# Output projection of the last two tile pairs by seven products, with the sums of w_o made in the second pass of keys and values

## The chip, the cores and the metric

The kernel runs on one core of a Trainium2 chip. TensorE (PE) multiplies, VectorE (DVE), ScalarE (ACT) and GpSimd (POOL) work on elements, and SyncE (SP) issues nearly all DMA transfers of the part that is changed. Each engine takes its own instructions in order, and engines wait for each other by semaphores. The metric is the device time of one execution in microseconds (us), as the median of several runs; lower is better.

## The reference

With B = 1, S = 2048 rows, D = 1024, H = 32 heads of 32 and a hidden width of 3584, all in float32:

```python
xn = layernorm(x)
q, k, v = heads(xn @ wqkv)
phi_q, phi_k = ([softmax(p), softmax(-p)] over the features of a head, p = q @ w_phi or k @ w_phi)
kv, z = sum over rows of phi_k^T v, sum over rows of phi_k          # per head
o = (phi_q @ kv) / (phi_q . z + 1e-6)
s = o.reshape(S, D) @ wo                                            # the output projection
B = (silu(xn @ w1) * (xn @ w3)) @ w2
return x + s * silu(B)
```

## The kernel before

**Products.** Every large product is made of float32 operands that are split in two: a cast to the rounded type (`hi`, on ACT) and the rest (`lo`, on DVE), both by `split`. A product of 128 rows by 512 columns takes three matmuls for each 128 of depth, `PASSES` = hi·hi, hi·lo, lo·hi. The hidden layer, the queries, keys and values and the w2 product go one step further: the matrices are cut in 2 x 2 blocks and multiplied in the manner of Strassen and Winograd, seven products of blocks in place of eight:

```python
ORDER = (("b", "A11", "B11"), ("a", "A12", "B21"), ("b", "S2", "T2"), ("c", "S1", "T1"),
         ("b", "S3", "T3"), ("c", "S4", "B22"), ("b", "A22", "T4"))
LAST = {"a": "A12", "b": "A22", "c": "S4"}
```

The first letter is the PSUM bank that a product adds to; `S1 = A21 + A22`, `S2 = S1 - A11`, `S3 = A11 - A21`, `S4 = A12 - S2`, and `T1` to `T4` are the like sums of the blocks of the other matrix (`b_sums` on POOL makes T2 and T3's source first). A bank is read between two products that add to it, so a product may have to wait for the copy of the sum so far. The 16 row tiles are worked in eight pairs.

**Stages, by the trace.** Layernorm and the hidden layer end at about 1132 us. Then come three passes over the eight pairs (`heads` twice, `queries` once; matmuls at L932, a pair takes 20.6 us): the first and second halves of keys and values, c=0 (1133 to 1297) and c=1 (1297 to 1464), and the queries, c=2 (1464 to 1617). In a pass each pair has seven products, and between them `steps()` issues side work: loads of the next pair's operands (`reload`), and in c=0 from the fifth product on `split_wo`, which loads the 16 blocks of w_o (128 x 512 each, two rooms, each with two places for a raw block and its split form), splits them and stores them to `wo_d`. A row `ev` is a feature or value tile of a pass, `k0` the copy of A11's part of a pair. The w2 product goes from 1617 to 2156 (L1338).

**The last stage** (2156 to 2351) is the output projection, in plain products: `wos[c, k]` holds the 16 split blocks of w_o, and for each of eight pairs b `half_out` makes the four quarters (row tile a, column half c), 24 matmuls each into one of three banks `pm`. Around these stand, for the pairs after it: `load_e`, `swap` (transposes of the features on DVE), `weigh`, `add_up`, `factors` and `weights` (denominators on POOL and DVE), `heads_out` (L1309, 128 small matmuls that make the next pair's o, transposed, in two PSUM tiles `po0` and `po1` of two banks each) and `operand` (casts and low parts of `po` to `oT`). `result(m, p)` handles the m-th quarter: multiply by the gate (L1484, DVE), add x (L1485, POOL, in the last quarter DVE), store, and load of the gate and x for three quarters later (`load_gx`, tile `gx`). Rows `late` are blocks of w_o that stand in a ring of other weights. Code is written out in the order in which each engine is to run it, and SP's queue takes its loads and stores in that order.

In the rows, a line number is that of the file's kernel; after the change it is 1 higher up to L1163, 25 higher in the second pass's loop, and 27 higher in the last stage up to L1492.

Of the kernel before, what the change touches and what calls it, by code (L numbers as in the profile page):

```python
# [17 lines left out]
P = 128  # L18
# [10 lines left out]
def tile_kernel(ctx: ExitStack, tc: tile.TileContext, x, wkT, wqT, wv, wphi, wo, w1, w3, w2, out):  # L29
# [8 lines left out]
    def close(*names):  # L38
        for name in names:
            open_pools.pop(name).__exit__(None, None, None)  # L40
# [39 lines left out]
    s_d = dram.tile([4, P, 2, P], F, name="s_d")  # L80
    zr_d = dram.tile([P, 2, 256], F, name="zr_d")
    wo_d = [[dram.tile([P, 2, 512], F, name=f"wo_d{c}_{k}") for k in range(ND)] for c in range(2)]
    w2_d = [{n: dram.tile([P, 2, 2, 512], F, name=f"w2_d{kb}{n}") for n in BNAMES} for kb in range(NKB)]
    kv_d = [dram.tile([P, 8, DH], F, name=f"kv_d{c}") for c in range(2)]
    kvu_d = dram.tile([P, 16, DH], F, name="kvu_d")
# [1065 lines left out]
    def split_wo(step):  # L1151

        if step == 0:
            wso["room"] = [big.tile([P, 8, 512], F, name="room", tag=f"big{j}") for j in range(2)]
        for m in range(16):
            room, at_ = wso["room"][m % 4 // 2], 3 * (m % 2)
            raw_w, two = room[:, at_], room[:, at_ + 1:at_ + 3].bitcast(R)
            c, k = m // 8, m % 8
            if step == 2 * m:
                nc.sync.dma_start(raw_w, wo[k * P:(k + 1) * P, c * 512:(c + 1) * 512])  # L1160
            elif step == 2 * m + 3:
                split(two[:, 0], two[:, 1], raw_w)
            elif step == 2 * m + 5:  # L1163
                nc.sync.dma_start(wo_d[c][k], two.bitcast(F))

    close("ps2")
    ps = pool("ps", 2, space=PSUM)
    BANKS = {"a": 2, "b": 3, "c": 2}
# [2 lines left out]
    for c in range(3):  # L1171
        wbn = {}
        if c == 2:
            in_order(ENG.SP, ENG.PE)
            close("spare")
            bpa = pool("ra", 1, side="right")
        for i in range(len(pairs)):
            nxt, end = {}, i + 1 == len(pairs)

            def steps():  # L1180
                for j in range(7):
                    if c == 0 and 4 <= 7 * i + j < 40:
                        split_wo(7 * i + j - 4)
                    if j == 0:
                        if i + 2 == len(pairs) and c < 2:
                            for m in range(2):
                                wbn.update(fetch(c + 3, m))
                        if c == 2 and i == 6:
                            nxt.update(reload(7, ANAMES[:3]))
                            ahead[0, 0] = load_h(0, 0)  # L1190
                            nxt.update(reload(7, ANAMES[3:]))
                        elif not (end and c == 2):
                            nxt.update(reload((i + 1) % len(pairs)))
                        if c == 2 and i in (1, 2):
# [295 lines left out]
    def weights(b):  # L1490

        scale(b, 0, nc.vector)  # L1492
        scale(b, 1, nc.gpsimd)

    load_gx(0)
    load_gx(1)
    load_e(2, 1)
    gate(*pairs[-1])
    load_gx(2)
    last = None  # L1500
    for b in range(NB):
        p0 = half_out(oT, 0, 0)
        if b == 0:
            add_up(1, 1)
# [27 lines left out]
        if b < 2:  # L1532
            if b == 0:
                heads_out([po[a // 2][:, a % 2] for a in range(4)])
            add_up(b + 2, 1)
            nxt = [operand(0, [(0, po[0]), (2, po[1])])]
            factors(b + 2)
            weights(b + 2)
            if b == 0:
                result(2, p2)  # L1540
            nxt.append(operand(1, [(0, po[0]), (2, po[1])]))
        else:
            if b + 2 < NB:
                weights(b + 2)
            if b + 1 < NB:
                nxt = [operand(t, [(0, po[0]), (2, po[1])]) for t in range(2)]
        if b + 2 < NB:
            for c in range(2 if b == 0 else 1):
                swap(b + 2, c)
                load_e(b + 4, c)  # L1550
# [5 lines left out]
        if b + 3 < NB:  # L1556
            add_up(b + 3, 0)
        oT = nxt
    result(4 * NB - 1, last)
    in_order()  # L1560
    close("ps4", "rb", "acc", "q", "work", "small", "misc", "ra", "rw", "edge_r", "edge_l")

# [37 lines left out]
```

## Time and profile before

| what | value |
|---|---|
| median of 3 runs | 2360.53 us (2357.38 to 2361.70) |
| the profiled execution | 2357.35 us, span 2355.2 us |
| PE busy | 2330.3 us, 99% of the span, 13298 matmuls |
| weight loads (PEld) | 1924.1 us, 82%, beside the matmuls |
| DVE busy | 1755.1 us, 75% |
| ACT busy | 861.2 us, 37% |
| POOL busy | 759.4 us, 32% |
| DMA | 588.93 MB, 250 GB/s in the mean |
| matmul clock granted | 1.0 in the run |

The span is the time from the first to the last record of the execution. An engine's busy time is that of its records; PE's matmuls overlap, so what one of them is worth is read from the starts of many in a row and not from the mean duration of a record. A row of a wait names the engine that waited, the tile that it was about to make, and the instruction or transfer that came last. Rows in order of time have the start, the length, the engine, the line, the operation, output<-input, and at the end in brackets the idle time ahead and its releaser.

### The profile page before, as it was taken

Reading aid. Unit: us, or ns where it says so; the run is one execution under the profiler, and the core shown is the slowest. Engines: PE = TensorE matmul, PEld = TensorE weight load, DVE = VectorE, ACT = ScalarE, POOL = GpSimd, SP = SyncE. Lnnn points to the kernel's source line nnn. Section 1 sums busy time; section 2 is a strip of 40 time slices with the busy share of each in tenths; the row PEclk is TensorE's granted clock in tenths of the full one; section 3 lists DMA queues with packets and bytes.
Section 4 is the critical chain, followed back from the end, with each engine's and each line's share of the span. In section 5 each row is a group of like instructions: output and inputs, shape, how many; then the busy total and the mean of one; then the engine's idle time right before and its main releaser. Section 6 shows DMA issues by size and latency. Waiting matters only on the chain. (4 is left out here: it accounts for less than half of the span.)

```text
span 2355.2 us, 35868 instructions
## 1 busy us (share of the span) xinstructions
PE 2330.3 (99%) x13298; PEld 1924.1 (82%) x13298; DVE 1755.1 (75%) x2531; ACT 861.2 (37%) x1535; POOL 759.4 (32%) x571
## 2 busy tenths in 40 slices
PE   7999999999999999999999999999999999999999
PEld 6888888888888888888888888888888888888877
DVE  8777877784688878885566656797678778888883
ACT  6544545443445444453221211234422222243100
POOL 2333545452455555552000000231011111115872
PEclk9999999999999999999999999999999999999999
DMA  5667699987877777776998877999444443367754
GB/s 188 212 217 248 217 331 334 310 295 224 271 269 256 256 272 280 264 265 225 367 337 341 320 243 272 356 346 314 150 148 167 179 179 124 118 253 294 246 184 133
DMA packets 320558, 588.93 MB, mean 250 GB/s; under 512 B 25728, under 2 KB 158336, under 8 KB 317696
## 3 DMA queue, kind: packets, MB, share of 16 engines
q1 hardware_dynamic: 305600, 571.96, 69.7%
q10 hardware_dynamic: 14784, 14.68, 1.8%
q8 instruction: 105, 1.72, 0.3%
q14 instruction: 69, 0.57, 0.1%
HBM read 380.76 MB, written 206.32 MB: 249 GB/s over the span
## 5 line engine op out<-in xcount | busy, mean ns | idle before, releaser
L344 DVE TENSOR_TENSOR bo<-rw,bo 128x512 fp32r<-128x512 f32 x332 | 309.0, 931 | 144.0 <-ACT bo L340 142.0
L1348 POOL TENSOR_TENSOR acc<-acc,u 128x512 f32<-128x512 f32 x48 | 63.0, 1312 | 450.6 <-ACT u L1347 442.9
L1338 PE MATMUL bankb<-bo,as 128*128 128x512 f32 x816 | 201.1, 389 | 0.4 <-DMA bo<-w_d0T 0.4
L340 ACT CAST bo<-rw 128x512 fp32r<-128x512 f32 x332 | 199.0, 617 | 5.5 <-DMA rw<-in_w 3.5
L1338 PEld LDWEIGHTS bankb<-bo,as 128*128 128x128 f32 x816 | 153.0, 188 | 32.6 <-DMA bo<-w_d0T 0.8
L1465 PE MATMUL pm<-wos,oT 128*128 128x512 f32 x720 | 166.9, 390 | 0.0
L703 PE MATMUL bankc<-op0S,bo 128*128 128x512 f32 x672 | 163.3, 392 | 0.9 <-DVE bo L344 0.5
L703 PE MATMUL bankb<-op0S,bo 128*128 128x512 f32 x672 | 162.8, 391 | 1.2 <-DVE bo L344 0.6
L703 PE MATMUL bankb<-op0A,bo 128*128 128x512 f32 x672 | 163.1, 392 | 0.0
L703 PE MATMUL bankb<-op1S,bo 128*128 128x512 f32 x672 | 161.4, 389 | 0.0
L703 PE MATMUL bankb<-op1A,bo 128*128 128x512 f32 x672 | 161.4, 389 | 0.0
L703 PE MATMUL bankc<-op1S,bo 128*128 128x512 f32 x672 | 161.4, 389 | 0.0
L1465 PEld LDWEIGHTS pm<-wos,oT 128*128 128x128 f32 x720 | 134.6, 188 | 30.6 <-issue 2.9
L703 PEld LDWEIGHTS bankc<-op1S,bo 128*128 128x128 f32 x672 | 126.2, 188 | 26.1
L703 PEld LDWEIGHTS bankb<-op1S,bo 128*128 128x128 f32 x672 | 126.2, 188 | 26.1
L703 PEld LDWEIGHTS bankb<-op1A,bo 128*128 128x128 f32 x672 | 126.2, 188 | 26.1
L703 PEld LDWEIGHTS bankb<-op0S,bo 128*128 128x128 f32 x672 | 125.3, 188 | 27.1 <-DVE bo L344 0.9
L703 PEld LDWEIGHTS bankc<-op0S,bo 128*128 128x128 f32 x672 | 125.1, 188 | 27.2 <-DVE bo L344 0.8
L1338 PE MATMUL bankc<-bo,as 128*128 128x512 f32 x576 | 146.2, 389 | 0.0
L703 PEld LDWEIGHTS bankb<-op0A,bo 128*128 128x128 f32 x672 | 125.0, 188 | 25.4
L129 POOL TENSOR_TENSOR rw<-rw 128x512 f32<-128x512 f32 x56 | 81.6, 1457 | 149.1 <-DMA rw<-in_w 129.2
L1350 DVE TENSOR_TENSOR acc<-bankb,acc 128x512 f32<-128x512 f32 x152 | 104.3, 686 | 32.7 <-PE bankb L1338 28.6
(262 smaller groups left out, 4708.4 us busy)
## 6 DMA issues: line engine op xcount, KB each, us to landing
rw<-in_w SPq DMA_DIRECT2D x224, 256.0 KB, 3.6
hr<-h_d SPq DMA_DIRECT2D x56, 512.0 KB, 4.0
xoS<-xo_d0S SPq DMA_DIRECT2D x48, 512.0 KB, 8.1
xoS<-xo_d1S SPq DMA_DIRECT2D x48, 512.0 KB, 6.8
xoA<-xo_d0A SPq DMA_DIRECT2D x36, 512.0 KB, 7.6
xoA<-xo_d1A SPq DMA_DIRECT2D x36, 512.0 KB, 6.1
e<-e_d SPq DMA_DIRECT2D x32, 512.0 KB, 5.6
h_d<-h SPq DMA_DIRECT2D x56, 256.0 KB, 4.6
```

The lines of the kernel that those rows point to most:

```text
L129: nc.gpsimd.tensor_sub(b12, b22, b12)
L340: nc.scalar.copy(bos[k, n][:, 0], raw_b(k, n).rearrange("p (k n) -> p k n", n=P))
L344: nc.vector.tensor_sub(b[:, 1], raw_b(k, n).rearrange("p (k n) -> p k n", n=P), b[:, 0].bitcast(F))
L703: nc.tensor.matmul(bank, bt[:, w, kk], aos[tb][an][:, u, kk], start=an in ("A11", "A12", "S1") and n == 0, stop=LAST[b] == an and n == 11, ...
L1338: nc.tensor.matmul(bank[b], t[:, u, pos + k], bos[kb, bn, k][:, w], start=first and n == 0, stop=LAST[b] == an and n == 5, skip_group_chec ...
L1348: nc.gpsimd.tensor_add(c, c, u)
L1350: nc.vector.tensor_add(c, pb, c)
L1465: nc.tensor.matmul(p, oT[a][k // 4][:, u, k % 4], wos[c, 4 * (k % 2) + k // 2][:, w], start=n == 0, stop=n == 23)
```

## The change

The last two pairs, b=6 and b=7, are projected by seven products of 12 matmuls (`product7`, depth 512, three passes) in place of four quarters of 24. The loop over pairs ends at b=5.

- `sum_wo`, in the second pass (c=1) from its fifth product on, one step to a product: for each of four blocks of the depth it loads four blocks of w_o, makes T2, T3, T1, T4 (POOL), splits each into `two`, one buffer of a room (`room[:, 5:7]`), and stores it to the new `wt_d`. Two rooms take turns by block.
- In the last stage 16 loads bring `wt_d` back: T2 to a ring and T1 and T3 to tiles of `accp` after b=4, after b=5 and in b=6, and T4 over w_o's own blocks of B12 (`reuse_b12`), which the seven products don't need.
- `raw_o` copies o from `po` to four tiles `ro` on ACT (L1547), `one` splits an operand to `o7`, `sums_o` makes S3, S1, S2 and the split of S2 on DVE, `rest_o` the splits of S1, S3, S4 and A22.
- Banks: three `pm` banks for b=6; for b=7 the tile `po0` holds the banks "b" and "a" and `po1` the bank "c".
- A product's end: A11's, S2's and S1's sums so far are copied to `part` (ACT, L1594); A12's, S3's and S4's are added to that (DVE) and go through `put`, which does what `result` does.

```diff
+    def sum_wo(step):
+        if step == 0:
+            wso["sums"] = [big.tile([P, 8, 512], F, name="room", tag=f"big{j}") for j in (5, 6)]
+        for k in range(4):
+            room, at_ = wso["sums"][k % 2], step - 8 * k
+            b11, b12, b21, b22, t2 = (room[:, j] for j in range(5))
+            two = room[:, 5:7].bitcast(R)
+            if at_ == 0:
...
+                        nc.sync.dma_start(room[:, 2 * a + c], wo[r0:r0 + P, c * 512:(c + 1) * 512])
+            elif at_ == 3:
+                b_sums(b11, b12, b22, t2)
+            elif at_ == 5:
+                nc.gpsimd.tensor_sub(b11, b22, t2)
+                nc.gpsimd.tensor_sub(b21, b21, t2)
+            for j, (n, src) in enumerate((("T2", t2), ("T3", b12), ("T1", b11), ("T4", b21))):
+                if at_ == 4 + 2 * j:
+                    split(two[:, 0], two[:, 1], src)
+                elif at_ == 5 + 2 * j:
+                    nc.sync.dma_start(wt_d[n][k], two.bitcast(F))
...
+                    if c == 1 and 4 <= 7 * i + j < 40:
+                        sum_wo(7 * i + j - 4)
...
+    def raw_o():
+        o = {}
+        for n, t, m in (("A11", 0, 0), ("A12", 0, 1), ("A21", 1, 0), ("A22", 1, 1)):
+            o[n] = work.tile([P, 4, P], F, name="ro", tag="w")
...
+            for c in range(2):
+                nc.scalar.copy(r5[:, :, c], src[:, :, c, t])
+        return o
...
+    def sums_o(ops, o):
+        o["S3"] = work.tile([P, 4, P], F, name="ro", tag="w")
+        nc.vector.tensor_sub(flat(o["S3"]), flat(o["A11"]), flat(o["A21"]))
+        o["S1"], o["S2"], o["S4"] = o["A21"], o["A11"], o["A12"]
+        nc.vector.tensor_add(flat(o["S1"]), flat(o["A21"]), flat(o["A22"]))
+        nc.vector.tensor_sub(flat(o["S2"]), flat(o["S1"]), flat(o["A11"]))
+        one(ops, o, "S2")
+    def rest_o(ops, o):
+        one(ops, o, "S1")
+        one(ops, o, "S3")
+        nc.vector.tensor_sub(flat(o["S4"]), flat(o["A12"]), flat(o["S2"]))
+        one(ops, o, "S4")
+        one(ops, o, "A22")
...
+    def product7(b, an, bn, ops, bank):
...
+                nc.tensor.matmul(bank, ops[an][:, u, k], w4[:, w], start=first and n == 0,
+                                 stop=LAST[BANK[an]] == an and n == 11, skip_group_check=True)
...
+        if an in ("A11", "S2", "S1"):
+            part[an] = work.tile([P, 512], F, name="part", tag="h1", bufs=2)
+            nc.scalar.copy(part[an], bank)
+        elif an == "A12":
+            nc.vector.tensor_add(part["A11"], bank, part["A11"])
+            put(4 * b, part["A11"])
...
-    for b in range(NB):
+    for b in range(NB - 2):
...
+        if b == 4:
+            for k in range(4):
+                load_t("T2", k, None)
+            load_t("T1", 0, None)
+            for k in (1, 2):
+                load_t("T1", k, k - 1)
+        if b == 5:
+            for n, k, tag in (("T1", 3, 2), ("T3", 0, 3), ("T3", 1, 8), ("T3", 2, 9)):
+                load_t(n, k, tag)
+    b = NB - 2
+    sums_o(ops, o)
...
+        product7(b, an, bn, ops, banks7[bk])
+        if an == "A11":
+            swap(b + 1, 1)
+            result(4 * b - 1, last)
+            load_gx(4 * b + 3)
+            rest_o(ops, o)
+            load_t("T3", 3, 10)
+            for k in range(4):
+                reuse_b12("T4", k)
+        elif an == "S1":
+            heads_out([po[a // 2][:, a % 2] for a in range(4)])
+            o2, ops2 = raw_o(), {}
+            one(ops2, o2, "A11")
+            one(ops2, o2, "A12")
+    sums_o(ops2, o2)
+    rest_o(ops2, o2)
+    b, last2 = NB - 1, [ps.tile([P, 2, 512], F, name=f"po{m}", bufs=1) for m in range(2)]
+    banks7 = {"b": last2[0][:, 0], "a": last2[0][:, 1], "c": last2[1][:, 0]}
+    for _, an, bn in ORDER:
+        product7(b, an, bn, ops2, banks7[BANK[an]])
```

Three places in the order of instructions show where the new work stands. ACT in the second pass, in the third pair: `k0` and the copies of `bankb` and `bankc` empty PE's banks, `ACTIVATE` is the exponential of the features. Before:

```order
L945 COPY k0_11536<-bankb_11523 128x512
L117 ACTIVATE ev_11472<-ev_11472 128x1024
L955 COPY ev_11642<-bankb_11523 128x16x32
L117 ACTIVATE ev_11642<-ev_11642 128x1024
L960 COPY ev_11668<-bankc_11655 128x16x32
L945 COPY k0_11732<-bankb_11719 128x512
```

And after the change, with `room` the cast of a sum:

```order
L946 COPY k0_11575<-bankb_11562 128x512
L118 ACTIVATE ev_11501<-ev_11501 128x1024
L94 CAST room_11307<-room_11307 128x512
L956 COPY ev_11686<-bankb_11562 128x16x32
L94 CAST room_11308<-room_11308 128x512
L94 CAST room_11307<-room_11307 128x512
L118 ACTIVATE ev_11686<-ev_11686 128x1024
L961 COPY ev_11714<-bankc_11701 128x16x32
L94 CAST room_11307<-room_11307 128x512
L946 COPY k0_11790<-bankb_11777 128x512
```

Four casts stand between the copies that PE's banks need. Three of them write the one buffer of room 11307, so each of these comes after the store of the one before.

ACT at the end of the program, where the last operands are made. Before:

```order
L93 CAST oT_20072<-po0_18512 128x2x128 x2
L93 CAST oT_20073<-po1_18513 128x2x128 x2
L93 CAST oT_20082<-po0_18512 128x2x128 x2
L93 CAST oT_20083<-po1_18513 128x2x128 x2
L93 CAST oT_20292<-po0_18512 128x2x128 x2
L93 CAST oT_20293<-po1_18513 128x2x128 x2
L93 CAST oT_20302<-po0_18512 128x2x128 x2
L93 CAST oT_20303<-po1_18513 128x2x128 x2
L1596 UNCONDITIONAL_BRANCH
```

After the change, from the first two copies of b=7's o on:

```order
L1547 COPY ro_20419<-po0_18610 128x2x128 x2
L1547 COPY ro_20422<-po1_18611 128x2x128 x2
L94 CAST o7_20425<-ro_20413 128x512
L94 CAST o7_20428<-ro_20416 128x512
L94 CAST o7_20491<-ro_20413 128x512
L94 CAST o7_20494<-ro_20419 128x512
L94 CAST o7_20497<-ro_20487 128x512
L94 CAST o7_20501<-ro_20416 128x512
L94 CAST o7_20504<-ro_20422 128x512
L1594 COPY part_20521<-po0_20507 128x512
L1594 COPY part_20551<-po0_20507 128x512
L1594 COPY part_20565<-po1_20508 128x512
```

The seven casts, of A11, A12, S2, S1, S3, S4 and A22, all stand ahead of the copy of A11's part out of the tile `po0`.

PE at the end, with its waits. Before, the last pair:

```order
L1465 MATMUL pm<-wos,oT 128x512 [waits DVE_49,Activation_49]
L1465 MATMUL pm<-wos,oT 128x512 x2
L1465 MATMUL pm<-wos,oT 128x512 [waits Activation_49]
L1465 MATMUL pm<-wos,oT 128x512 x8
L1465 MATMUL pm<-wos,oT 128x512 [waits Activation_49]
L1465 MATMUL pm<-wos,oT 128x512 x2
L1465 MATMUL pm<-wos,oT 128x512 [waits Activation_49]
L1465 MATMUL pm<-wos,oT 128x512 x8
L1465 MATMUL pm<-wos,oT 128x512 [waits DVE_49]
L1465 MATMUL pm<-wos,oT 128x512 x20
L1465 MATMUL pm<-late,oT 128x512 x3
```

After, the first five products of b=7 (A11, A12, S2, S1, S3):

```order
L1589 MATMUL po_20507<-wos,o_20425 128x512 [waits PE_49,Activation_49]
L1589 MATMUL po_20507<-wos,o_20425 128x512 x11
L1589 MATMUL po_20507<-wos,o_20428 128x512 [waits Activation_49]
L1589 MATMUL po_20507<-wos,o_20428 128x512 x11
L1589 MATMUL po_20507<-late,o_20491 128x512 [waits DVE_49]
L1589 MATMUL po_20507<-late,o_20491 128x512 x8
L1589 MATMUL po_20507<-wt,o_20491 128x512 x3
L1589 MATMUL po_20508<-wt,o_20494 128x512 [waits PE_49]
L1589 MATMUL po_20508<-wt,o_20494 128x512 x11
L1589 MATMUL po_20507<-wt,o_20497 128x512 [waits Activation_49]
L1589 MATMUL po_20507<-wt,o_20497 128x512 x11
```

A12's first matmul (`o_20428`) waits for ACT, and S2's (`o_20491`) for DVE; the tile `po_20507` holds the banks of both.

More of the change, by code (lines that the diff above doesn't have):

```diff
@@ L82, in tile_kernel @@
     wo_d = [[dram.tile([P, 2, 512], F, name=f"wo_d{c}_{k}") for k in range(ND)] for c in range(2)]
+    wt_d = {n: [dram.tile([P, 2, 512], F, name=f"wt_d{n}_{k}") for k in range(4)] for n in ("T1", "T2", "T3", "T4")}
     w2_d = [{n: dram.tile([P, 2, 2, 512], F, name=f"w2_d{kb}{n}") for n in BNAMES} for kb in range(NKB)]
@@ L1164, in split_wo @@
                 nc.sync.dma_start(wo_d[c][k], two.bitcast(F))
+    def sum_wo(step):
[6 more added lines that the diff above has]
+            if at_ == 0:
+                for a in range(2):
+                    r0 = (4 * (k % 2) + 2 * a + k // 2) * P
+                    for c in range(2):
[10 more added lines that the diff above has]
+                    nc.sync.dma_start(wt_d[n][k], two.bitcast(F))
     close("ps2")
@@ L1493, in weights, with load_t, reuse_b12, b_of @@
         scale(b, 1, nc.gpsimd)
+    wt = {}
+    def load_t(n, k, tag):
+        t = ring("wt") if tag is None else accp.tile([P, 2, 512], R, name="wt", tag=f"acc{tag}")
+        nc.sync.dma_start(t.bitcast(F), wt_d[n][k])
+        wt[n, k] = t
+    def reuse_b12(n, k):
+        t = wos[1, 4 * (k % 2) + k // 2]
+        nc.sync.dma_start(t.bitcast(F), wt_d[n][k])
+        wt[n, k] = t
+    def b_of(bn, k):
+        if bn in wt_d:
+            return wt[bn, k]
+        return wos[int(bn[2]) - 1, 4 * (k % 2) + 2 * (int(bn[1]) - 1) + k // 2]
@@ new lines, in raw_o, with one @@
+    def raw_o():
+        o = {}
+        for n, t, m in (("A11", 0, 0), ("A12", 0, 1), ("A21", 1, 0), ("A22", 1, 1)):
+            o[n] = work.tile([P, 4, P], F, name="ro", tag="w")
+            r5 = o[n].rearrange("p (b c) (r u) -> p b c r u", c=2, u=4)
+            src = po[m].rearrange("p b (c t u r) -> p b c t r u", c=2, t=2, u=4)
+            for c in range(2):
+                nc.scalar.copy(r5[:, :, c], src[:, :, c, t])
+        return o
+    def one(ops, o, n):
+        ops[n] = quad("o7")
+        split(ops[n][:, 0], ops[n][:, 1], o[n])
@@ new lines, in put @@
+    def put(m, src):
+        (b, a, c), t = halves[m], gx.pop(m)
+        nc.vector.tensor_mul(t[:, 0], src, t[:, 0])
+        (nc.vector if m + 2 == len(halves) else nc.gpsimd).tensor_add(t[:, 0], t[:, 0], t[:, 1])
+        r0 = SETS[b][a] * P
+        nc.sync.dma_start(out[r0:r0 + P, c * 512:c * 512 + 512], t[:, 0])
+        if m + 4 < len(halves):
+            load_gx(m + 4)
+    part = {}
+    def product7(b, an, bn, ops, bank):
+        first = an in ("A11", "A12", "S1")
+        n = 0
+        for k in range(4):
+            w4 = b_of(bn, k)
+            for u, w in PASSES:
+                nc.tensor.matmul(bank, ops[an][:, u, k], w4[:, w], start=first and n == 0,
+                                 stop=LAST[BANK[an]] == an and n == 11, skip_group_check=True)
+                n += 1
+        if an in ("A11", "S2", "S1"):
[4 more added lines that the diff above has]
+            put(4 * b, part["A11"])
+        elif an == "S3":
+            nc.vector.tensor_add(part["S1"], bank, part["S1"])
+            put(4 * b + 3, part["S1"])
+        elif an == "S4":
+            nc.vector.tensor_add(part["S2"], bank, part["S2"])
+            put(4 * b + 1, part["S2"])
+        else:
+            put(4 * b + 2, bank)
@@ L1544, in tile_kernel @@
                 weights(b + 2)
-            if b + 1 < NB:
+            if b + 3 < NB:
                 nxt = [operand(t, [(0, po[0]), (2, po[1])]) for t in range(2)]
+            else:
+                o, ops = raw_o(), {}
+                one(ops, o, "A11")
+                one(ops, o, "A12")
         if b + 2 < NB:
@@ L1558, in tile_kernel @@
         oT = nxt
-    result(4 * NB - 1, last)
+        if b == 4:
[9 more added lines that the diff above has]
+    sums_o(ops, o)
+    banks7 = {}
+    for _, an, bn in ORDER:
+        bk = BANK[an]
+        if bk not in banks7:
+            banks7[bk] = ps.tile([P, 512], F, name="pm", tag="mm", bufs=3)
+        product7(b, an, bn, ops, banks7[bk])
[5 more added lines that the diff above has]
+            load_t("T3", 3, 10)
+            for k in range(4):
+                reuse_b12("T4", k)
[8 more added lines that the diff above has]
+    banks7 = {"b": last2[0][:, 0], "a": last2[0][:, 1], "c": last2[1][:, 0]}
+    for _, an, bn in ORDER:
+        product7(b, an, bn, ops2, banks7[BANK[an]])
     in_order()
```

## The prediction

> **What bounds the kernel now.** I read the page first, then the waits of PE, then the order of time in the two places that the change touches.
>
> ```profile
> span 2355.2 us, 35868 instructions
> PE 2330.3 (99%) x13298; PEld 1924.1 (82%) x13298; DVE 1755.1 (75%) x2531; ACT 861.2 (37%) x1535; POOL 759.4 (32%) x571
> PE 31%; DMA 1%; issue 0%; DVE 0%; POOL 0%; ACT 0%; POOLq 0%; DVEq 0%; ACTq 0%
> PE bankc L932 <- issue: 1.2, 1, 1.2
> ```
>
> PE is busy for 99% of the span, the chain of waits is PE's, and outside the opening no wait of PE is over 1.2 us (last row). So a matmul less is worth its own time, and a wait that is put on PE costs all of its length. The profiled execution took 2357.35 us, 2.15 above its span and 3.18 below the median of the runs, 2360.53; sums below are made against this execution and then set on the median. 0.2% is 4.7 us, about what a measurement of this kernel tells from no change.
>
> The last two pairs, b=6 and b=7, in order of time:
>
> ```profile
> 2304.24 10.36 PE L1465 MATMUL pm<-wos,oT 128*128 128x512 f32 x45
> 2315.21 2.76 PE L1309 MATMUL po<-et,kvt 32*32 32x256 f32 x128
> 2317.90 10.50 PE L1465 MATMUL pm<-wos,oT 128*128 128x512 f32 x45
> 2328.91 10.36 PE L1465 MATMUL pm<-wos,oT 128*128 128x512 f32 x45
> 2339.79 10.36 PE L1465 MATMUL pm<-wos,oT 128*128 128x512 f32 x45
> 2349.99 0.84 PE L1465 MATMUL pm<-late,oT 128*128 128x512 f32 x3
> 2350.93 0.69 DVE L1484 TENSOR_TENSOR gx<-pm,gx 128x512 f32<-128x512 f32 x1 [4.75 <-PE pm L1465]
> 2351.65 0.69 DVE L1485 TENSOR_TENSOR gx<-gx 128x512 f32<-128x512 f32 x1
> ```
>
> 48 matmuls (45 on `wos`, 3 on `late`) lie between 2328.91 and 2339.79: 0.2267 us each, 2.72 for a product of 12. PE doesn't pause, and `heads_out` of the last pair moves the next start from 2315.12 (2304.24 plus 48 x 0.2267) to 2317.90: 2.78.
>
> **The matmuls saved.** Two pairs by seven products of 12 take 168 matmuls in place of 192: 24 x 0.2267 = **5.44 us less**. That is the most that the change can give; nothing after the last product changes (multiply, add, store).
>
> **The last pair's new waits.** The order shows the place: ACT's seven casts of the last pair stand ahead of its copy of A11's part. The banks of this pair are two tiles `po0` (products "b" and "a") and `po1` ("c"); the built program makes the first matmul of A12 wait for ACT and the first of S2 for DVE, and their semaphore counts are those of that copy and of A12's own eviction, since all four touch the tile `po0`. S2 would have to wait for the copy anyway (same bank); A12, a product ahead of it, waits because of the tile alone. What the copy waits for, in durations:
>
> ```profile
> 1355.15 2.88 PE L932 MATMUL bankc<-op3B,xoS 128*128 128x512 f32 x12
> 1357.87 2.88 PE L932 MATMUL bankb<-op3T,xoA 128*128 128x512 f32 x12
> 1358.07 0.69 DVE L964 TENSOR_TENSOR ev<-bankc,ev 128x512 f32<-128x512 f32 x1 [1.96 <-PE bankc L932]
> 1297.57 0.69 DVE L111 TENSOR_REDUCE mm<-bankb 128x16 f32<-128x512 f32 x1 [2.03 <-PE bankb L932]
> 1298.18 0.68 DVE L112 TENSOR_REDUCE mm<-bankb 128x16 f32<-128x512 f32 x1
> L93 ACT CAST as<-s 128x512 fp32r<-128x512 f32 x15 | 9.3, 620 | 43.4 <-DVE s L1143 43.4
> L94 DVE TENSOR_TENSOR as<-s,as 128x512 fp32r<-128x512 f32 x15 | 10.4, 692 | 0.3
> L344 DVE TENSOR_TENSOR bo<-rw,bo 128x512 fp32r<-128x512 f32 x332 | 309.0, 931 | 144.0 <-ACT bo L340 142.0
> ```
>
> A product's eviction starts 2.92 after the product (1355.15 to 1358.07); DVE's operations on 128x512 start 0.60 apart, 0.70 where one needs the one before; a cast takes 0.62 and a low part 0.69 (0.93 in the row where POOL also works). Call the start of b=6's A22 zero. Six products and `heads_out` lie before it, so it is 2304.24 + 16.32 + 2.78 = 2323.34. A11 of b=7 goes from 2.72, A12 wants 5.44. On DVE A22's multiply starts at 2.92, then S3 at 3.5, S1 at 4.1, S2 at 4.8 to 5.5 (it needs S1). ACT casts S2 from 5.55 to 6.17; DVE makes the low parts of S2, S1, S3 from 6.2, 6.8, 7.4 and the sum S4 from 8.0 to 8.7. ACT, which has cast S1 and S3 meanwhile, casts S4 from 8.75, A22 from 9.3, and copies A11's part from 9.8 to 10.4. So A12 starts at 10.45 and not 5.44: **5.0 us of waiting**. Its eviction starts 2.92 later, at 13.4, and ends at 14.1; S2 starts there, not at 13.2: **0.9 more**. S1, S3, S4 and A22 follow at 16.8, 19.5, 22.3, 25.0, and the last multiply at 27.9, on the clock of the trace 2351.2 against 2350.93: **+0.3**. With POOL's additions beside DVE's first sums (0.93 for 0.69, twice) it is +0.8; if DVE and ACT overlap more than I let them, -0.5. I take +0.4, since as many rows lie at 0.69 as POOL has additions there.
>
> **b=6 itself** doesn't wait, by the same steps. Raw copies and casts of its first two operands stand where the casts of `operand` stood:
>
> ```profile
> 2293.35 0.37 ACT L93 CAST oT<-po 128x256 fp32r<-128x256 f32 x1 [15.98 <-PE po L1309]
> 2318.03 0.37 ACT L93 CAST oT<-po 128x256 fp32r<-128x256 f32 x1 [17.00 <-PE po L1309]
> 2318.89 0.65 ACT L93 CAST oT<-po 128x256 fp32r<-128x256 f32 x2 [0.49 <-DVE oT L94]
> ```
>
> Eight of these 0.28 apart (two take 0.65) and two casts end 3.5 after `heads_out`; DVE has the first sum of S2 ready by 2304.6, S2's product wants it at 2309.7. For b=7 the same work ends on DVE at 2322.3, and S3's eviction behind it at 2322.9, under A22's start of 2323.34: cover 0.4, and 0.3 of waiting if the low parts take 0.93. I set 0.
>
> **The 16 loads of the sums** (512 KB each) go on SP's queue, seven after b=4's results, four after b=5's, five in b=6; PE needs them from 2309.7. The latest is the fourth of T3: it stands behind a load that has to wait until result 23 is stored, since both use one buffer. That result's multiply comes behind the transposes, at about 2307.7; then
>
> ```profile
> L1485 POOL TENSOR_TENSOR gx<-gx 128x512 f32<-128x512 f32 x31 | 39.7, 1294 | 54.9 <-DVE gx L1484 35.9 <-DMA gx<-in_x 16.1 <-DMA e<-e_d 2.0
> out<-gx SPq DMA_DIRECT2D x32, 256.0 KB, 2.3
> wo_d<-room SPq DMA_DIRECT2D x16, 512.0 KB, 8.2
> wo_d<-room SPq DMA_DIRECT2D x1, 512.0 KB, 2.8
> ```
>
> 0.7 + 1.3 + 2.3 and two issues: it is issued at 2312.5 and lands 2.8 to 8.2 later, 2315 to 2320.7, wanted at 2317.9 + 9 x 0.2267 = 2319.9. At the long end it is 0.8 late; the queue is idle then, so I take 0.
>
> **The second pass (c=1)** gets 16 splits (16 casts of 0.62 on ACT, 16 low parts on DVE), 16 POOL sums, 16 loads and 16 stores. Room for the work there is:
>
> ```profile
> 1236.00:1256.00 20.00, 20.00 (x211) 16.46 (x210) 12.77 (x18) 3.92 (x6) 0.26 (x2) 1.00 0.95 361
> 1380.00:1400.00 20.00, 20.00 (x211) 16.47 (x210) 12.31 (x17) 3.79 (x5) 0.26 (x2) 1.00 0.59 182
> ACT room L93 <- DMA room<-in_wo: 24.0, 12, 5.8
> ```
>
> (Columns: window, its length, busy PE, PEld, DVE, ACT, POOL, clock, DMA share, GB/s.) In a pair's 20.6 us DVE works 12.3 and ACT 3.8; the new work adds about 2.2 and 2 to a pair. The first pass carries 16 splits of `wo` already, with ACT waiting 24.0 us for their loads, and PE lost there only the 1.2 us of the first fence. But the new splits write one buffer per room, so a cast has to wait until the split before it is stored, and ACT takes its instructions in order. Where that hurts is the third pair:
>
> ```profile
> 1343.42 1.06 ACT L117 ACTIVATE ev<-ev 128x1024 f32<-128x1024 f32 x1
> 1346.26 0.34 DVE L120 RECIPROCAL r<-r 128x32 f32<-128x32 f32 x1
> 1350.45 1.06 ACT L117 ACTIVATE ev<-ev 128x1024 f32<-128x1024 f32 x1 [0.72 <-DVE ev L115]
> 1352.70 0.59 ACT L960 COPY ev<-bankc 128x512 f32<-128x512 f32 x1 [1.19 <-PE bankc L932]
> 1163.74 0.45 SPq L1160 DMA_DIRECT2D room<-in_wo  x1
> 1174.78 0.32 SPq L1164 DMA_DIRECT2D wo_d<-room  x1
> ```
>
> T3 of the first block is cast after the exponential of 1343.42, its low part made after the reciprocal of 1346.26, its store issued near 1347.4. T1's cast waits for that store; behind it stand the exponential (1.06) and the copy of S1's bank (0.59), which the product of 1355.15 needs. So a landing over 1355.15 - 1347.4 - 0.62 - 1.06 - 0.59 = 5.4 us makes PE wait. In the first pass the stores took 8.2 in the median, but those that SP had been waiting to issue (nothing issued from 1163.74 to 1174.78) landed in 2.8; the new ones are of this kind. The Trainium skill ("DMA: Bandwidth & Descriptors", Queues, rings and completion order) says that each engine consumes a ring's descriptors in order; the 2.8 beside 8.2 agrees, and by it a store in an idle queue isn't held up by the loads issued behind it. Bounds: 0, and three such places (T1 of the first three blocks) at 8.2 - 5.4: 8.4. I take 0.3, nearest to the 2.8.
>
> **Sum:** -5.44 + 5.9 of waits, which is +0.4 with the rounding of the ends, +0.3 = +0.7, on the median 2361.2.
>
> **Rivals.**
> Slower: *stores on ACT's path* in the second pass, as just priced: from a landing of 5.4 us on, up to +8.4, with the rest 2369.6. For it speaks the 8.2; against it the 2.8 and that DMA is at 0.59 there.
> *PE's clock.* A wait of 5 us might let the clock fall. The trace has:
>
> ```profile
> 10.81 1.95 PE L225 MATMUL pt<-ident,xt 128*128 128x128 f32 x8 [10.81 <-DVE xt L219]
> 14.52 5.05 PE L225 MATMUL pt<-ident,xt 128*128 128x128 f32 x24 [1.76 <-DVE xt L219]
> 36.09 1.03 PE L225 MATMUL pt<-ident,x_room 128*128 128x128 f32 x8
> 38.35 1.09 PE L225 MATMUL pt<-ident,x_room 128*128 128x128 f32 x8 [1.23 <-ACT xf L230]
> ```
>
> After 10.8 us idle, 32 transposes took 7.0 us where 8 take 1.03 later (32: 4.1), while 1.23 us of waiting changed nothing. Half speed for a while costs at most the 2.9 between them: 2364. A wait of 5.0 lies between 1.23 and 10.8. The Trainium skill ("TensorE: Matmul & The Clock Gate", Part 1) has the array at half clock after an idle window of about 3.4 us; its windows run freely, so a wait of 5.0 would hold a whole one in about half of the cases (an estimate from that page).
> *Faster:* A12 doesn't wait for the copy after all. Then S2 waits from 8.16 to 10.45, 2.3 in place of 5.9: -3.1, 2357.7; with no wait at all -5.4, 2355.1. Against it stand the semaphore counts.
>
> **Chances.** The waits take the gain, within -1 and +2.5: 0.56. The clock falls as well: 0.18, about 2364. Stores on ACT's path: 0.18, most of it beyond 4.7. A12 free: 0.08, half of that without S2's wait. Faster by over 0.2% needs nearly all of the 5.44: 0.04; slower: 0.18 and a little of the clock's case, 0.2; within: 0.76. The range goes from A12 free (2357.5) to the stores' middle (2367).
>
> **What would show it.** In the profile after: 24 matmuls fewer at the end; in b=7 PE idle 4.5 to 5.5 us ahead of A12's product, released by ACT's copy, and 0.9 ahead of S2's, released by DVE; the last multiply within 1 us of 27.6 behind b=6's A22; no wait of PE over 1 us between 1297 and 1464. Waits of PE there for ACT's copies, or matmuls 0.43 apart behind the long wait, would make the prediction wrong upwards; no wait ahead of A12 downwards.

## The result and the profile after

The changed kernel takes 2377.39 us (median of 4 runs, 2375.47 to 2381.58) against 2359.26 before (2357.38 to 2361.70): the ratio is 1.0079, interval 1.0061 to 1.0096. It is slower by 18.1 us where I forecast 2361.2 and a range up to 2367.0. The profiled execution took 2376.87, 1.77 above its span.

The first rows of the page:

```profile
span 2375.1 us, 36003 instructions
PE 2332.7 (98%) x13274; PEld 1922.9 (81%) x13274; DVE 1787.2 (75%) x2559; ACT 880.1 (37%) x1571; POOL 786.4 (33%) x587
```

The 24 matmuls are gone (13298 to 13274), yet PE is busy 2.4 us longer: some of its matmuls ran slow. The waits of PE (what waited, released by what: us in total, times, longest), without those of the opening that were there before:

```profile
PE po L1589 <- ACT part L1594: 5.9, 1, 5.9
PE pm L1589 <- DMA wt<-wt_dT: 4.0, 1, 4.0
PE pkv L918 <- DVE ev L126: 3.6, 1, 3.6
PE bankc L933 <- ACT d L1074: 1.7, 2, 1.5
PE bankb L933 <- DMA xoA<-xo_d0A: 1.5, 1, 1.5
...
PE bankb L933 <- DVE ev L963: 0.9, 2, 0.5
...
PE po L1589 <- DVE part L1596: 0.9, 1, 0.9
```

Before, no wait outside the opening was over 1.2 us. The first and the last row are the two that I forecast. To see what each is worth I took the length of each stage from the start of its first matmul to that of the next stage (the last: to the end of PE's last matmul):

| stage | before | after | difference |
|---|---|---|---|
| up to the second pass | 1297.37 | 1297.05 | -0.3 |
| second pass (c=1) | 166.95 | 174.00 | +7.05 |
| queries (c=2) | 154.56 | 159.48 | +4.92 |
| w2 product | 537.32 | 536.17 | -1.15 |
| pairs b=0 to 5 | 148.04 | 148.07 | 0.0 |
| pairs b=6 and 7 | 46.59 | 55.91 | +9.32 |

The sum is +19.85, and the spans differ by 19.9. (The w2 product takes 536.2 to 537.5 in all the runs below, whatever the kernel; the second pass 174.0 here and 173.3 to 173.5 in three more runs with the same sums.) The last two pairs, in order of time:

```profile
2328.43 2.34 PE L1589 MATMUL pm<-wt,o 128*128 128x512 f32 x9
2334.77 1.65 PE L1589 MATMUL pm<-wt,o 128*128 128x512 f32 x3 [4.01 <-DMA wt<-wt_dT]
2336.22 2.96 PE L1589 MATMUL pm<-wos,o 128*128 128x512 f32 x9
...
2342.44 2.88 PE L1589 MATMUL po<-wos,o 128*128 128x512 f32 x12
2351.24 4.68 PE L1589 MATMUL po<-wos,o 128*128 128x512 f32 x12 [5.92 <-ACT part L1594]
2356.77 2.35 PE L1589 MATMUL po<-late,o 128*128 128x512 f32 x9 [0.85 <-DVE part L1596]
2358.95 6.29 PE L1589 MATMUL po<-wt,o 128*128 128x512 f32 x27
```

S3 of b=6 stands after 9 of its 12 matmuls, for T3's fourth load; A12 of b=7 waits 5.92 for the copy of A11's part. Behind each of the two waits matmuls are slow: A12's 12 take 4.68 where A11's took 2.88. From the start of b=6 (2314.77) to that of the last product (2367.80) lie 53.03 us; 13 products of 2.72 and `heads_out` of 2.78 are 38.15. So 14.9 were lost, against 5.4 saved: 10.8 in waits and 4.1 around them, about 3.5 of that in slow matmuls (the rest is the overlap of a product's start with the end of the one before, which a wait takes away).

In the second pass the largest loss stands in the fourth pair:

```profile
1355.20 2.88 SPq L599 DMA_DIRECT2D xoS<-xo_d0S  x4
1360.29 0.80 SPq L1189 DMA_DIRECT2D wt_dT<-room  x2
1370.24 0.62 ACT L94 CAST room<-room 128x512 fp32r<-128x512 f32 x1 [4.73 <-DMA wt_dT<-room]
1370.89 0.69 DVE L95 TENSOR_TENSOR room<-room 128x512 fp32r<-128x512 f32 x1 [3.52 <-ACT room L94]
1371.50 0.35 DVE L121 RECIPROCAL r<-r 128x32 f32<-128x32 f32 x1
1372.31 1.21 DVE L126 TENSOR_TENSOR ev<-ev,r 128x1024 f32<-128x1024 f32 x1
1373.66 0.76 PE L918 MATMUL pkv<-ev 128*32 128x34 f32 x64 [3.60 <-DVE ev L126]
1374.35 4.62 PE L933 MATMUL bankc<-op3T,xoS 128*128 128x512 f32 x12
```

A cast (T3 of the second block) waits for the store of T2, the second of the two issued from 1360.29 on, behind 2 MB of `xoS` loads. VectorE's low part waits for the cast, the reciprocal and multiply of the features stand behind the low part on VectorE, and PE wants the features. Two rows of the transfers give the landing of the stores: the 16 of the pass in the median, and the median of the two issued at 1360. The second of these, issued at 1360.66, is the one that the cast waits for: it took 9.6.

```profile
wt_dT<-room SPq DMA_DIRECT2D x16, 512.0 KB, 4.2
wt_dT<-room SPq DMA_DIRECT2D x2, 512.0 KB, 9.0
```

The queries' pass has no line of the change in it. But here, unlike in the last stage, VectorE, ScalarE and GpSimd run in an order that a planner makes from its own estimates of times, and it made another one: of 196 instructions of VectorE in this pass 27 stand elsewhere, of ScalarE's 86 five, of GpSimd's 32 two. VectorE in the first pair, before and after the change:

```profile
1483.05 0.69 DVE L1078 TENSOR_TENSOR d<-bankc,d 128x512 f32<-128x512 f32 x1
1483.78 0.69 DVE L996 TENSOR_REDUCE tops<-d 128x16 f32<-128x512 f32 x1
1484.73 1.22 DVE L1006 TENSOR_REDUCE s_all<-eq 128x32 f32<-128x1024 f32 x1 [0.26 <-ACT eq L1001]
1485.87 0.68 DVE L997 TENSOR_REDUCE mm<-d 128x16 f32<-128x512 f32 x1
```

```profile
1489.79 0.69 DVE L1079 TENSOR_TENSOR d<-bankc,d 128x512 f32<-128x512 f32 x1
1491.47 1.22 DVE L1007 TENSOR_REDUCE s_all<-eq 128x32 f32<-128x1024 f32 x1 [0.99 <-ACT eq L1002]
1492.60 0.68 DVE L997 TENSOR_REDUCE tops<-d 128x16 f32<-128x512 f32 x1
1493.20 0.68 DVE L998 TENSOR_REDUCE mm<-d 128x16 f32<-128x512 f32 x1
```

`tops` now stands behind a sum that waits for ScalarE, so the minimum, from which GpSimd and ScalarE go on, comes 3.41 behind the addition from `bankc` in place of 2.82. A pair later PE waits 1.50 for ScalarE's copy of `bankc`, and 1.50 for a load of `xoA` that SyncE issued later.

### The profile page after: what moved, and what is told of

It is laid out like the page before. It is cut to its first block, busy times and chain, and to the rows that moved or that the text cites. A ratio compares the mean times of both kernels' runs of the same rounds, so it can differ in the third digit from the quotient of the medians.

```text
span 2375.1 us, 36003 instructions
## 1 busy us (share of the span) xinstructions
PE 2332.7 (98%) x13274; PEld 1922.9 (81%) x13274; DVE 1787.2 (75%) x2559; ACT 880.1 (37%) x1571; POOL 786.4 (33%) x587
## 5 line engine op out<-in xcount | busy, mean ns | idle before, releaser
L1365 PEld LDWEIGHTS bankc<-bo,as 128*128 128x128 f32 x576 | 108.1, 188 | 22.5
L1492 PE MATMUL pm<-wos,oT 128*128 128x512 f32 x540 | 125.3, 391 | 0.0
L1377 DVE TENSOR_TENSOR acc<-bankb,acc 128x512 f32<-128x512 f32 x152 | 104.2, 686 | 26.4 <-PE bankb L1365 22.6
```

What stands on the lines that cost most here:

```text
L1365: nc.tensor.matmul(bank[b], t[:, u, pos + k], bos[kb, bn, k][:, w], start=first and n == 0, stop=LAST[b] == an and n == 5, skip_group_chec ...
L1377: nc.vector.tensor_add(c, pb, c)
L1492: nc.tensor.matmul(p, oT[a][k // 4][:, u, k % 4], wos[c, 4 * (k % 2) + k // 2][:, w], start=n == 0, stop=n == 23)
```

## The experiments

All are compared with the kernel before on the same chip. "Second pass", "queries" and "last two pairs" are differences in length from the profile of before, as in the table above.

**Which part costs.** Two runs split the change. The sums alone are the changed kernel's `sum_wo` in the kernel before, with `wt_d` stored and not read:

```diff
+                    if c == 1 and 4 <= 7 * i + j < 40:
+                        sum_wo(7 * i + j - 4)
```

> The kernel before, with the sums of w_o made, split and stored in the second pass and never read; the projection is as before. Theory: the loss ahead of the last stage is all due to this work: the second pass 7.0 us longer (the largest single wait of PE 3.6 in the fourth pair, behind a cast that waits for a store), the queries' pass 4.8 longer, the w2 product 1.1 shorter: 2359.3 + 10.7 = 2370. Rival: the loads and operands of the last stage share the blame (through the queue or through the order of instructions): under 5 us in all, 2364 or less.

2366.78 against 2357.08, ratio 1.0038 (1.0023 to 1.0053), so 9.7 us. Second pass +6.3, queries +3.9. The second part alone:

```diff
-                    if c == 1 and 4 <= 7 * i + j < 40:
-                        sum_wo(7 * i + j - 4)
+    wt_d = {n: [wo_d[m // 2][4 * (m % 2) + k] for k in range(4)] for m, n in enumerate(("T1", "T2", "T3", "T4"))}
```

> The changed kernel without the sums of w_o: the 16 loads of the last stage read split blocks of w_o in their place, so the projection of the last two pairs has wrong weights and the same instructions. Theory: nothing changes ahead of the last stage (within 0.5 us), and the last two pairs lose 14.9 us in waits and slow matmuls (T3's load 4.0, A11's copy 5.9, A12's eviction 0.9, clock 4.1) against 5.4 saved: 2359.3 + 9.4 = 2368.7. Rival: T3's late load follows from the second pass being late; then it is not there, and the run takes 2363.

2367.55 against 2357.08, ratio 1.0040 (1.0025 to 1.0055): 10.5 us. Second pass +0.1, queries -0.2, last two pairs +10.6, with T3's wait of 3.4 and A12's of 5.9. The two parts add up (9.7 + 10.5 = 20.2 against 18.1 +- 4), and the last stage's loss doesn't come from the passes ahead of it.

**What holds the second pass.** Two edits of the sums alone that take the store away from ScalarE. In the first each sum has places of its own in the room:

```diff
-            for j, (n, src) in enumerate((("T2", t2), ("T3", b12), ("T1", b11), ("T4", b21))):
+            for j, (n, src, lo, hi) in enumerate((("T2", 4, 5, 6), ("T3", 1, 1, 7), ("T1", 0, 0, 4), ("T4", 2, 2, 3))):
...
-                    split(two[:, 0], two[:, 1], src)
+                    split(room[:, hi].bitcast(R), room[:, lo].bitcast(R), room[:, src])
...
-                    nc.sync.dma_start(wt_d[n][k], two.bitcast(F))
+                    nc.sync.dma_start(wt_d[n][k], room[:, lo:hi + 1:hi - lo])
```

> Run of the sums alone, but each of the four sums of a block is split to places of its own in the room (the low part over the sum, the cast in a free place), so no cast waits for the store ahead of it in its block. The order of instructions in the queries' pass is the changed one, not that of before. Theory: the second pass loses under 2 us in place of 7; the queries' pass still loses 4 to 5, because its loss comes from the changed order on VectorE: 2359.3 + 5 = 2364. Rival 1: the stores are not what holds ACT, but the added work and loads: the second pass loses 7 again. Rival 2: the queries' pass loses because it starts with a backlog from the second: it loses under 1.

2370.85, ratio 1.0054 (1.0037 to 1.0070). The second pass lost 10.3, more than with one buffer; the queries 3.7. My theory was wrong for the second pass: freed from the stores, the planner put the four casts of a block together, in the third pair three of them ahead of the copy of `bankc`, where one waited 2.4 for GpSimd's sums. In the second edit GpSimd issues the stores:

```diff
-                    nc.sync.dma_start(wt_d[n][k], two.bitcast(F))
+                    nc.gpsimd.dma_start(wt_d[n][k], two.bitcast(F))
```

> Run of the sums alone, with the 16 stores issued by GpSimd on a queue of its own in place of SyncE's. One buffer as in the change. The order of instructions in the queries' pass is that of before. Theory: a store on SyncE's queue stands behind the loads of the next pair's operands (2.5 MB); on a queue of its own it lands in under 5.4 us, so the second pass loses under 3, and the queries' pass under 1: 2361 to 2362. Rival: the landing is set by the traffic as a whole, not by the queue: the casts wait 4 to 5 us again and the second pass loses 7.

2384.60, ratio 1.0116 (1.0101 to 1.0131). The stores landed in 4.8 in the median, under 5.4 as I had it, and yet the second pass lost 26.4. GpSimd issued every store within 1.3 of its low part, so the issue isn't what is late; but here too the planner made another order. The second cast of the first block now stands ahead of the copy to `k0`, and the casts wait for landings of 3.4 to 8.1. PE's longest wait, 7.4, stands behind a landing of 6.5 and then a cast, a low part, the reciprocal and the multiply of the features. Since the order changed with each of the two edits, neither shows what the buffer or the queue alone is worth. The queries lost nothing (-0.2).

The third edit leaves buffer, steps and queue as in the change, and moves the casts and low parts:

```diff
-                    split(two[:, 0], two[:, 1], src)
+                    nc.gpsimd.tensor_copy(two[:, 0], src)
+                    nc.gpsimd.tensor_sub(two[:, 1], src, two[:, 0].bitcast(F))
```

> Run of the sums alone with one edit: the cast and the low part of each sum are made by GpSimd; steps, the one buffer of a room and the stores on SyncE's queue are those of the change, and so is the order of the queries' pass. Theory: in the changed kernel TensorE waits in the second pass because VectorE and ScalarE stand, in their own order, behind casts and low parts that wait for a store; with these on GpSimd, which has next to nothing else to do there, the second pass loses under 2 us in place of 6 to 7, and the queries' pass its 4 to 6 as before: 4 to 8 over before. Rival: the stores delay SyncE's loads of the next pair, which stand behind them: TensorE waits for xoA or xoS in the second pass and it loses 4 or more.

2366.93 against 2358.01, ratio 1.0033 (1.0023 to 1.0044). The second pass lost 2.1 in place of 6.3. Most of what is left are waits of 1.0 and 0.5 for `xoA` and `xoS`, which the rival had at 4 or more. So about 4 of the 6.3 us go with the casts and low parts standing on ScalarE and VectorE, where the rows above show them waiting for a landing. The queries lost 6.7, and so the run 8.9, a little over the 4 to 8 that I had.

The fourth has casts, low parts and stores on GpSimd, places as in the first edit, 12 steps to a block, and the memsets of the values' last columns on VectorE:

```diff
-            room, at_ = wso["sums"][k % 2], step - 8 * k
+            room, at_ = wso["sums"][k % 2], step - 12 * k
...
+                    nc.gpsimd.tensor_copy(room[:, hi].bitcast(R), room[:, src])
+                    nc.gpsimd.tensor_sub(room[:, lo].bitcast(R), room[:, src], room[:, hi])
...
+                    nc.gpsimd.dma_start(wt_d[n][k], room[:, lo:hi + 1:hi - lo])
```

> The kernel before with the sums of w_o in the second pass and nothing of them on ScalarE, VectorE's low parts or SyncE's stores: casts, low parts and stores on GpSimd, each sum in places of its own, 12 steps a block; the memsets of the values' last columns go to VectorE. The order of instructions in the queries' pass is that of before. Theory: what made TensorE wait was ScalarE and VectorE standing behind loads, sums and stores: the second pass loses under 1.5 us, the queries' pass nothing: within 2 us of before. Rival: GpSimd's 48 operations slow VectorE's beside them (0.68 to over 1 us, as in the changed kernel's trace) and TensorE waits for evictions: 3 to 7 us.

2359.12 against 2357.68, ratio 1.0007 (0.9998 to 1.0015). Second pass +0.7, queries 0.0: the same loads, sums and stores cost next to nothing in the median where no engine of the critical path stands behind them.

**What costs the queries' pass.** One edit of that run, the stores on SyncE's queue again:

```diff
-                    nc.gpsimd.dma_start(wt_d[n][k], room[:, lo:hi + 1:hi - lo])
+                    nc.sync.dma_start(wt_d[n][k], room[:, lo:hi + 1:hi - lo])
```

> The run of the sums on GpSimd with one edit: its 16 stores go on SyncE's queue again. With that the order of the queries' pass on VectorE, ScalarE and GpSimd is exactly that of the changed kernel (27 rows of VectorE moved against before). Theory: the queries' pass loses 4 to 5 us from its order alone, with two waits of 1.5 us in the second pair (ScalarE's copy of bankc, a load of xoA), though the second pass loses under 2: 4 to 6 over before. Rival: the queries' pass lost because it began with a backlog of the second pass: then it loses under 1 here, and the run is within 2 of before.

2363.64 against 2357.77, ratio 1.0023 (1.0014 to 1.0032). Second pass +0.2, queries +6.0, with the two waits in the second pair that the changed kernel has:

```profile
1501.28 3.01 PE L933 MATMUL bankc<-op4B,xoS 128*128 128x512 f32 x12 [1.09 <-ACT d L1074]
1504.13 2.88 PE L933 MATMUL bankb<-op4T,xoA 128*128 128x512 f32 x12
1509.15 4.46 PE L933 MATMUL bankb<-op4B,xoA 128*128 128x512 f32 x12 [2.14 <-DMA xoA<-xo_d0A]
```

The backlog is refuted twice: here the second pass loses nothing and the queries 6.0; with GpSimd's stores from one buffer it lost 26.4 and the queries nothing. What goes with the loss is the order. Over all kernels, those with the changed order lost 3.7 to 6.8 in the queries' pass (seven runs), those with that of before -0.2 to 0.0 (six). The order of VectorE, ScalarE and GpSimd and that of SyncE's loads changed together in every one of them, so how the loss divides between them stays open. All seven also have the 16 stores on SyncE's queue, and the six don't; that the order and not the stores themselves costs the time is argued and not shown. For it speaks that in the last run the last store landed 23 us before the queries' pass began.

**The last stage.** First A12's bank alone, in the changed kernel:

```diff
-    banks7 = {"b": last2[0][:, 0], "a": last2[0][:, 1], "c": last2[1][:, 0]}
+    banks7 = {"b": last2[0][:, 0], "a": ps.tile([P, 512], F, name="pm", tag="mm", bufs=3), "c": last2[1][:, 0]}
```

> The changed kernel with the bank of A12 in b=7 in a tile of its own (one of the three pm banks). Theory: A12 waited for the copy of A11's part because of the tile alone. It now follows A11 at once, and S2, which needs the bank, waits for that copy instead, 3.3 us (copy ended at 2351.2, S2 wanted at 2347.9) in place of 5.9 and 0.9: 5.6 us less than the changed kernel with the slow matmuls, or 4 less if 3.3 us of waiting still slows the matmuls behind it: 12.5 to 14 us over before. Rival: A12's product is held by the copy itself (ScalarE reads while TensorE writes) or by the weights: nothing moves.

2375.78 against 2357.68, ratio 1.0074 (1.0061 to 1.0087). A12 (first row) follows A11 at once, and S2 waits 3.20 for the copy:

```profile
2350.58 2.88 PE L1589 MATMUL pm<-wos,o 128*128 128x512 f32 x12
2356.66 3.13 PE L1589 MATMUL po<-late,o 128*128 128x512 f32 x9 [3.20 <-ACT part L1594]
2359.59 7.21 PE L1589 MATMUL po<-wt,o 128*128 128x512 f32 x27
```

So the tile alone made A12 wait. From A11's start to PE's end b=7 takes 24.4 in place of 28.2, the 4 us that I gave for the case that matmuls stay slow. The whole run is 18.1 over before and not 12.5 to 14, because T3's load was 4.8 late here and the queries lost 6.8 in place of 4.9. Next, three edits together (the bank, and these two):

```diff
     sums_o(ops2, o2)
-    rest_o(ops2, o2)
...
         product7(b, an, bn, ops2, banks7[BANK[an]])
+        if an == "A11":
+            rest_o(ops2, o2)
...
             swap(b + 1, 1)
+            load_t("T3", 3, 10)
             result(4 * b - 1, last)
             load_gx(4 * b + 3)
             rest_o(ops, o)
-            load_t("T3", 3, 10)
```

> The changed kernel with three edits in the last stage: A12's bank apart; in b=7 the splits of S1, S3, S4 and A22 written behind A11's product, so that the copy of A11's part comes ahead of them on ScalarE; T3's fourth load ahead of result 23 on SyncE's queue. Theory: the waits of 4.0, 5.9 and 0.9 and the slow matmuls behind them (4.1) are all that the last two pairs lost: the stage is 5.4 us shorter than before, and the run 14.9 shorter than the changed kernel: 3 us over before. Rival: DVE is what is late in b=7 (sums and low parts); then S2 or S1 still wait 2 to 5 us.

2367.98, ratio 1.0041 (1.0028 to 1.0054): 10.3 over before and not 3. All three waits are gone and b=7 runs through, but the last two pairs are 0.6 longer than before and not 5.4 shorter: A22 of b=6 now waits 2.2 for T4's loads, the next in SyncE's queue, and about 3.5 are lost in slow matmuls behind it. So the waits were not all that the last two pairs could lose. Both mends in one kernel (the sums of the run on GpSimd, this last stage):

> The changed kernel with both mends: the sums as in the run on GpSimd, the last stage as mended. Theory: the 24 matmuls saved come through, and the second pass costs 0 to 2: 3.4 to 5.4 us under before. Rival: the second pass takes 3 to 7: within 2 us of before or over it.

2357.32 against 2357.68, ratio 1.0004 (0.9994 to 1.0014), where I had 3.4 to 5.4 under before. Second pass +0.6, queries -0.2, last two pairs -0.5, again with A22 behind T4. Two more orders of SyncE's queue were tried on it, T4 ahead of everything of b=6, and T4 right behind T3's fourth (in both the two lines are taken out of their old place behind `rest_o`):

```diff
     sums_o(ops, o)
+    for k in range(4):
+        reuse_b12("T4", k)
```

> The run with both mends, and T4's four loads issued ahead of b=6's first product in place of behind result 23 and T3's last load. In that run b=6's A22 waited for T4 (2.2, 0.2 and 0.4 us) and 3 of its matmuls ran slow. Theory: no wait of TensorE over 1 us is left in the last two pairs, the 24 matmuls come through whole, and the sums cost 0.5 to 1.5: 4 to 5 us under before. Rival: a next transfer or VectorE's operands of b=7 come late in its place: 1 to 2 under before.

```diff
             load_t("T3", 3, 10)
+            for k in range(4):
+                reuse_b12("T4", k)
             result(4 * b - 1, last)
```

> The run with both mends, and T4's four loads directly behind T3's fourth, ahead of result 23 (in that run they stood behind it and cost 2.8 us and some slow matmuls; ahead of everything they made T3's fourth load 3.3 late). Theory: no wait of TensorE over 1 us is left in the last two pairs and the last matmul comes 5.4 us earlier than before against the pass ahead of it; with the 0.5 to 1.5 of the sums the run is 4 to 5 under before. Rival: VectorE's multiplies in the second pass now and then take several us beside GpSimd, as in the run with T4 ahead (9.8 for 1.2): the median is under 2 below before.

I had 4 to 5 under before for each. With T4 ahead of everything 2358.15 against 2357.77, ratio 1.0004 (0.9995 to 1.0013): T3's fourth load was 3.3 late, and the last two pairs are 0.65 shorter than before. With T4 behind T3 2359.50 against 2358.01, ratio 1.0011 (0.9999 to 1.0024), last two pairs +1.3: no load of a sum was late, and b=6 ran through, but S2 of b=7 waited 3.9:

```profile
2328.79 0.69 DVE L1573 TENSOR_TENSOR gx<-part,gx 128x512 f32<-128x512 f32 x1 [4.35 <-DMA gx<-g_d]
2335.74 0.62 ACT L94 CAST o<-ro 128x512 fp32r<-128x512 f32 x1 [12.71 <-DVE ro L1560]
2336.89 4.21 PE L1589 MATMUL po<-late,o 128*128 128x512 f32 x9 [3.87 <-ACT part L1594]
```

Now the gate's loads stand behind 4.5 MB of sums; VectorE's multiply of a result waits 4.35 for one, and the sums of b=7, behind it on VectorE, come late. So the wait that T3's load had went to T4's, back to T3's, and to the gate's. No version tried is faster than the kernel before by more than can be told.

## Why the prediction was wrong

**The matmuls saved** (-5.44): right, 24 x 0.2267, and nowhere cashed in full, since the last two pairs never ran without a wait.

**The last pair's waits** (+5.9): right in mechanism, place and nearly in size. A12 waited 5.92 where I had 5.0, S2 0.85 where I had 0.9; the tile as cause is shown. I had the last multiply 27.9 behind A22 of b=6 (the 27.6 among the signs is its place before the change); it came 31.1 behind it, and two thirds of the 3.2 are slow matmuls.

**PE's clock** was a rival with 0.18 and at most 2.9. It came, behind each of the three longest waits (3.6, 4.0 and 5.9), 1.5 to 2.1 at a time: it should have been a surcharge on every long wait of the sum and not a case beside it. In b=6 and 7 alone it cost about 3.5. The granted clock of the profile shows it: it is 0.5 for 3.41 us from 1375.2 and from 2334.4 on, for 6.83 from 2348.0 on, and 1.0 at every other time from behind the opening to the last matmul.

**The loads of the sums** (0, with 0.8 at the long end): wrong, 4.0 and 1.5 of slow matmuls. The step that failed is the issue of T3's fourth load "at 2312.5", which is 2323.0 on the changed kernel's clock. The rows:

```profile
2321.72 0.65 DVE L1511 TENSOR_TENSOR gx<-pm,gx 128x512 f32<-128x512 f32 x1
2324.15 0.34 SPq L1514 DMA_DIRECT2D out<-gx  x1
2328.64 0.32 SPq L1505 DMA_DIRECT2D gx<-g_d  x1
2329.53 0.38 SPq L1526 DMA_DIRECT2D wt<-wt_dT  x1
```

The multiply of result 23 came 3.5 later than I had it, since on VectorE the sums of b=6 and the transposes stand ahead of it; the store took 4.5 to free the tile for the next load and not 2.3, the median of all such stores before the change; and the load, issued at 2329.53, landed after 5.2, within the 2.8 to 8.2 that I gave.

**The second pass** (+0.3, bounds 0 and 8.4): wrong, +7.05. The failing choice was the 2.8 us of a store in an idle queue. The queue isn't idle: `reload` puts 3.5 MB of operands on it in every pair. The first three stores, up to the third pair, which I had worked out, did land in 3.0 to 4.1; the store that mattered, in the fourth, landed in 9.6. I also followed only ScalarE, in the third pair; the largest wait came in the fourth, on VectorE, whose reciprocals stand behind a low part that waits for the cast. That 7.05 lies under the upper bound of 8.4 is luck: the bound was three landings on ScalarE's path in the first three blocks, and the loss was a wait of 3.6 on VectorE's path, 1.6 of slow matmuls behind it and shorter waits.

**The queries' pass** (not in the sum): +4.92. I put this pass at nothing without a reason: I took the order of instructions as changed only where the diff has lines, and the order of this pass is set by a planner.

**The chances.** I gave the stores on ScalarE's path and the clock as cases that exclude each other, and T3's load none of its own. They came together, with one more that I hadn't: 7.05 + 4.92 + 9.32 against +0.7.

## What to carry to other kernels

Where a planner orders the instructions, compare the order of the stages behind the edit too: with 16 added stores 27 instructions of a pass that has no edit moved, and the runs with that order lost 4 to 7 us there. Side work was nearly free only on an engine behind which nothing of the critical path stands; the same 64 casts, sums, low parts and stores cost their pass 0.2 to 26 us by where they were put. On a core that is 99% busy, price each wait by its length plus the slow matmuls that may follow it, and a transfer by its landing in the queue as it will be then.

## What the runs showed of the hardware

Matmuls can run slow behind much shorter waits than I had bounded (between 1.23 and 10.8 us), and the length of the wait alone doesn't decide it. Two rows from the run with places of its own, and one from the run with T4 ahead:

```profile
1358.01 4.59 PE L933 MATMUL bankc<-op3B,xoS 128*128 128x512 f32 x12 [1.83 <-ACT ev L961]
1382.03 3.01 PE L933 MATMUL bankc<-op3B,xoS 128*128 128x512 f32 x12 [1.57 <-ACT ev L961]
2333.44 0.97 PE L1589 MATMUL pm<-wt,o 128*128 128x512 f32 x3 [3.33 <-DMA wt<-wt_dT]
```

A wait of 1.83 made the matmuls behind it 1.7 us longer, and one of 1.57 did nothing. One of 3.33 did nothing either: its three matmuls took 0.97, where the same three took 1.65 behind the wait of 4.01 in the changed kernel. The granted clock tells these apart, and it is the clock that makes the matmuls slow. Two windows of the changed kernel (the clock stands third from the end), the first with the two waits of 1.50 in the queries' pass, the second with that of 4.01:

```profile
1480.00:1520.00 40.00, 36.15 (x218) 28.96 (x217) 26.08 (x37) 12.07 (x16) 5.65 (x6) 1.00 0.93 325
2330.00:2340.00 10.00, 5.99 (x21) 4.54 (x20) 2.76 (x5) 2.48 (x8) 1.29 (x2) 0.83 0.97 329
```

In all runs the clock is 1.0 or 0.5. While the work goes on, it stays at 0.5 for 3.41, 6.83 or 10.24 us at a time, and in each run these stretches begin whole multiples of 3.41 us apart. Laid on that grid, behind the opening, the clock fell after every step of 3.41 in which PE had been idle for 1.83 us or more, and after none with 1.73 or less; at 1.77 it fell once and once not. The wait of 3.33 falls 1.63 and 1.70 on two steps, and one of 2.52 in the run of the sums alone 1.38 and 1.14. So which waits of 1.8 to 3.4 us are hit depends on where they fall. Where the clock fell, a wait cost 1.5 to 2.8 us more than its length, and 3.5 in one case of two waits close together. The Trainium skill ("TensorE: Matmul & The Clock Gate", Part 1) puts half clock behind an idle window of about 3.4 us; the half and the length agree with these rows, but a step didn't have to be idle as a whole, 1.83 of its 3.41 were enough.

One multiply of VectorE beside GpSimd's work on 128x512 tiles took 9.80 us where it takes 1.21, in the profiled execution of the run with T4 ahead:

```profile
1388.48 9.80 DVE L126 TENSOR_TENSOR ev<-ev,r 128x1024 f32<-128x1024 f32 x1
1398.42 1.13 PE L918 MATMUL pkv<-ev 128*32 128x34 f32 x64 [7.97 <-DVE ev L126]
```

That execution was the longest of its kernel (2366.32; the others 2356.71 to 2362.78). With sums and stores on GpSimd 5 of 46 executions lie 8 to 11 us above the median of their kernel, of the kernel before none over 6.6; of the five only this one has a trace. The Trainium skill ("GPSIMD Engine Reference", 1) says that GpSimd's way to SBUF is shared with VectorE's instructions of two SBUF inputs, which this one is. In the other runs it took 2.7 at most, and what made it 9.80 stays open.
